# Spectral gating kernel: exchanging the spectra of two neighbouring steps in one pair of transfers

## The chip, the core and the metric

One core of one Trainium2 chip runs the kernel. The metric is the device time of one execution in microseconds (us), from the runs that are shown; three runs of the kernel before gave 118.08, 118.17 and 118.53, median 118.17.

## What is computed

The input x has 2048 rows and 1024 columns in bfloat16. Two global filters A and B are applied to it in the frequency domain, and a gate for each row mixes the two results:

```python
x = A_x                                          # [1, 2048, 1024]
g = sigmoid((x * gate_w).sum(-1, keepdims=True))
X = rfft2(x)                                     # over rows and columns, 513 columns kept
a = irfft2(X * (A_w_r + 1j * A_w_i), s=(2048, 1024))
b = irfft2(X * (B_w_r + 1j * B_w_i), s=(2048, 1024))
out = g * a + (1 - g) * b
```

Only A's x is used. Each of the four filter tensors is [2048, 513] in bfloat16.

## The kernel before

All transforms are matrix products with constant cosine and sine tables on TensorE (PE). The 2048-point transform over rows is split into 32 times 64 points.

- **Stage 1** (`stage1`, L379 and L390) makes the 32-point part, after DVE has folded x (`fold`, L340).
- **Steps 0 to 15** (`step`) take the rest of the forward transform, each for one half of the columns and two of 16 blocks of row frequencies (steps 0 to 2 and 4 to 8 the lower half, 3 and 9 to 15 the upper). `stage2(i + 2)` makes the column transform two steps ahead (PE L451 and L460, copied out of PSUM by ACT L469 or, for two steps, by DVE L467). `stage4(i)` makes the 64-point transform over rows (PE L480), and ACT L487 writes the step's spectrum to tile XF. The real and imaginary parts of one frequency lie in neighbouring partitions.
- **`swap(i)`** exchanges neighbouring partitions: two DMAs copy the spectrum from XF to tile MM, one moves even partitions to odd ones, the other odd to even, 64 rows of 2048 bytes (128 KB) each. Steps 0 to 8 issue them from POOL, steps 9 to 15 from SP. A DMA is issued through the helper `dma`, so that all are recorded at L283.
- **`product(i, kind)`** (DVE L508) multiplies the spectrum with the filters, in place in tile W. Kinds A0 and A1 read the spectrum in XF, kinds B0 and B1 the exchanged one in MM. The digit is the filter, 0 or 1. Steps 7, 8 and 11 to 15 are taken in two halves of their columns, and 11 to 14 two steps at a time.
- **Row groups** (`group`, PE L604, copied out by ACT L615 or DVE L613) take eight columns each and start the inverse transform over rows. The first ones need the products of all steps of the lower half, of which step 8 is the last, and of its columns only the first half.
- **Stages 6 and 7** (PE L754 and L783) finish the inverse, and the rows are stored.

XF holds 8 spectra in a ring, MM holds 7 exchanged ones. Step i has place (i + 1) modulo 8 in XF and place (i + 1) modulo 7 in MM. Each place has a key in the program's own dependency tracking: `r` names what an instruction reads, `w` what it overwrites, `a` what it adds to; waits are derived from these keys. All DMAs with one name share a semaphore, and whoever reads what they wrote waits for all of them. Every engine runs its instructions in the order in which the program adds them.

A step calls `stage4(i)`, then `swap(i)`, then `stage2(i + 2)`; then the products of that step's entry in `ORDER` are added. The order of products on DVE is written out by hand. Entry by entry from step 3 on it is: A0 of 3, A0 of 2 | B0 of 0, A0 of 4, A1 of 0 | B0 of 1, B1 of 0, A1 of 1 | B0 of 2, B1 of 1, A1 of 2 | B0 of 3, B1 of 2, A1 of 3 | B0 of 4, B1 of 3, A1 of 4 | A0 and B0 of 5, B1 of 4, A1 of 5 | A0 and B0 of 6, B1 of 5, A1 of 6 | first half of the columns of 7, with B1 of 6 in between | first half of 8, then the second halves of 7 and 8 | 9.

The filters are loaded from HBM by SP (`wload`, 44 DMAs at L283, the last of them for steps 8 and 15). SP issues them ahead of its own exchanges, without waits in between, and after the exchanges come the constants of the later stages. POOL issues nothing but the exchanges of steps 0 to 8 in this part of the kernel.

Of the kernel before, what the change touches and what calls it, by code (L numbers as in the profile page):

```python
# [232 lines left out]
def bass_gated_mix__spectral_gfnet__spectral_gfnet__prompt_kernel(nc, A_x, A_w_r, A_w_i, B_x, B_w_r, B_w_i, gate_w, out):  # L233
# [9 lines left out]
    XF = sb("XF", 11264)  # L243
    MM = sb("MM", 7168)
# [13 lines left out]
    def sl(t, off, dims, p0=0, np_=128, pstep=1):  # L258
        n = t.shape[1]
        return AP(t, p0 * n + off, [[n * pstep, np_]] + [list(x) for x in dims])  # L260
# [4 lines left out]
    def bank(b):  # L265
        return ("ps", b)
# [15 lines left out]
    def dma(eng, name, dst, src, **kw):  # L282
        return P.add(eng, lambda e: e.dma_start(dst, src), dma=name, **kw)  # L283
# [11 lines left out]
    for _ in range(18):  # L295
        P.add("pe", lambda e: e.matmul(ps(7 * 512, [(1, 256)]), sl(CL, GRo, [(1, 128)]), sl(CL, GRo, [(1, 256)]), start=True, stop=True),
              r=["GRz"], w=[bank(7)])
# [114 lines left out]
    last1 = [P.ops["pe"][-1]]  # L412
    SEQ = [(0, 0), (0, 1), (0, 2), (1, 0)] + [(0, p) for p in range(3, 8)] + [(1, p) for p in range(1, 8)]
    CSo = lambda i: (i % 3) * 1024
    Xk = lambda i: (i + 1) % NX
    Xo = lambda i: 3072 + Xk(i) * 1024
    XSk = lambda i: (i + 1) % NXS
    XSo = lambda i: XSk(i) * 1024
# [70 lines left out]
        return out  # L489

    def swap(i):
        eng = ("pool", "sp")[i > 8]
        for ri in range(2):
            dma(eng, f"xs{i}", sl(MM, XSo(i), [(1, 1024)], p0=1 - ri, np_=64, pstep=2), sl(XF, Xo(i), [(1, 1024)], p0=ri, np_=64, pstep=2),
                r=[("X", Xk(i))], **({"a": [("XS", XSk(i))]} if ri else {"w": [("XS", XSk(i))]}), after=last1)

    def product(i, kind, h0=0, n=2, ni=1):

# [147 lines left out]
    def step(i):  # L646
        nonlocal last2
        stage4(i)()
        swap(i)
        if i + 2 < 16:  # L650
            last2 = stage2(i + 2)
# [45 lines left out]
    groups(1)  # L697
    out15()
    swap(15)
    groups(1)  # L700
    star_column(2 * spare())
# [224 lines left out]
```

## Time and profile before

| | us |
|---|---|
| median of three runs | 118.17 |
| the profiled execution | 118.88 |
| its span, first to last instruction | 116.6 |
| PE busy | 110.0 |
| DVE busy | 100.7 |
| ACT busy | 96.5 |
| POOL busy | 34.0 |
| median from issue to landing, exchanges from POOL (18 DMAs) | 5.4 |
| median from issue to landing, exchanges from SP (14 DMAs) | 2.7 |

The mean granted clock of TensorE was 0.991. Times in what follows are us from the start of the span. A group's line gives the line of the kernel, engine, operation, tiles (out<-in) and shapes. An engine's name with a q (SPq, POOLq) is its sequencer, which waits and issues DMAs. Queue 0 holds the DMAs that POOL issues, queue 1 those of SP. A wait in square brackets is idle time of the engine just before the instruction, with what ended it. In the timeline, neighbouring instructions of one group are merged (x2), and the length is that of all of them together.

### The profile page before, as it was taken

The page shows a single profiled execution, that of the slowest core. Times are in us where ns is not written, and L with a number is a line of the kernel's source. Part 1 is how long each engine was busy: PE and PEld are TensorE (multiplying, and loading weights), DVE is VectorE, ACT ScalarE, POOL GpSimd, SP SyncE. Part 2 cuts the span into 40 slices and gives each one's busy share as a digit, 9 for nine tenths or more (in the row PEclk, how much of TensorE's full clock was granted, in tenths as well). Part 3 has the DMA queues.
Part 4 walks back from the last instruction along what each step waited for, and adds up shares of the span by engine and source line. Part 5 has one row for each costly group of instructions (what it writes and reads, how often), then busy time and mean ns, then how long its engine had stood idle before and what let it go on. Part 6 is the DMA issues. An engine that isn't in the chain of part 4 may idle for free.

```text
span 116.6 us, 4237 instructions
## 1 busy us (share of the span) xinstructions
PE 110.0 (94%) x1812; PEld 88.4 (76%) x1812; DVE 100.7 (86%) x210; ACT 96.5 (83%) x117; POOL 34.0 (29%) x43
## 2 busy tenths in 40 slices
PE   6999999999999999999999999999999999999950
PEld 4666888875766657569999999999988777777430
DVE  0478998978999999699999999999568999899990
ACT  5239998997799999939999999997879889988420
POOL 1000030016655600000000000000002999999930
PEclk9999999999999999999999999999999999999996
DMA  3999999999999999962369930000000135425466
GB/s 86 289 405 415 421 359 355 352 349 350 363 370 358 368 364 362 350 241 100 139 172 407 389 123 0 6 0 6 0 6 0 46 146 181 181 96 193 153 233 236
DMA packets 17682, 26.14 MB, mean 224 GB/s; under 512 B 2112, under 2 KB 11072, under 8 KB 17664
## 3 DMA queue, kind: packets, MB, share of 16 engines
q1 hardware_dynamic: 16368, 23.00, 56.2%
q0 software_dynamic: 864, 2.36, 5.6%
q10 hardware_dynamic: 432, 0.52, 1.4%
q8 instruction: 14, 0.23, 0.8%
q14 instruction: 4, 0.03, 0.1%
HBM read 17.48 MB, written 4.19 MB: 186 GB/s over the span
## 4 chain that ended last, share of the span: by engine, by line
PE 51%; SPq 29%; DMA 9%; DVE 3%; issue 2%; ACT 2%; DVEq 0%
SPq L283 29%; PE PS L604 26%; PE PS L783 15%; PE PS L754 7%; DMA W<-in_B_w_i_dram 6%; DMA W<-in_A_x_dram 3%; PE PS L379 2%; DVE W L508 1%; DVE MM L794 1%; ACT W L615 1%; PE PS L563 1%; ACT XF L790 1%; PE PS L582 1%; DVE XF L340 0%; DVEq L865 0%
## 5 line engine op out<-in xcount | busy, mean ns | idle before, releaser
L604 PE MATMUL PS<-CL,W 128*128 128x128 bf16 x512 | 32.3, 225 | 0.2 <-DVE W L508 0.2
L604 PEld LDWEIGHTS PS<-CL,W 128*128 128x128 bf16 x512 | 31.6, 145 | 0.9 <-DVE W L508 0.7
L835 POOL TENSOR_TENSOR MM<-FT 128x512 bf16<-128x512 f32 x14 | 17.4, 1273 | 48.7 <-DVE FT L830 48.7
L615 ACT ACTIVATE W<-PS 128x1024 bf16<-128x1024 f32 (+1 forms) x30 | 28.5, 1036 | 3.0 <-PE PS L604 2.9
L508 DVE TENSOR_TENSOR W<-XF,W 128x1024 bf16<-128x1024 bf16 (+1 forms) x38 | 22.4, 608 | 1.6 <-DMA W<-in_B_w_i_dram 0.9
L508 DVE TENSOR_TENSOR W<-MM,W 128x1024 bf16<-128x1024 bf16 (+1 forms) x38 | 22.4, 613 | 0.2
L783 PE MATMUL PS<-FT,W 128*128 128x256 bf16 (+1 forms) x132 | 19.4, 299 | 0.1
L487 ACT ACTIVATE XF<-PS 128x1024 bf16<-128x1024 f32 x16 | 17.3, 1079 | 1.6 <-PE PS L480 1.6
L480 PE MATMUL PS<-XF,CK 128*128 128x512 bf16 (+1 forms) x72 | 17.8, 357 | 0.1
L767 ACT ACTIVATE W<-PS 128x1024 bf16<-128x1024 f32 (+1 forms) x15 | 14.8, 992 | 2.7 <-PE PS L754 2.7
L340 DVE TENSOR_TENSOR XF<-W 128x512 bf16<-128x512 bf16 (+2 forms) x34 | 11.4, 404 | 5.9 <-DMA W<-in_A_x_dram 5.7
L783 PEld LDWEIGHTS PS<-FT,W 128*128 128x128 bf16 x132 | 12.1, 98 | 5.4 <-DVE XF L794 0.7
L379 PE MATMUL PS<-MM,XF 128*128 128x256 bf16 x128 | 14.9, 273 | 0.6 <-DVE XF L340 0.4
L469 ACT ACTIVATE XF<-PS 128x1024 bf16<-128x1024 f32 x14 | 15.0, 1078 | 0.1
L379 PEld LDWEIGHTS PS<-MM,XF 128*128 128x128 bf16 x128 | 12.2, 98 | 3.5 <-DVE XF L340 2.0
L390 ACT ACTIVATE FT<-PS 128x1024 bf16<-128x1024 f32 (+2 forms) x15 | 13.1, 1012 | 0.8 <-PE PS L379 0.8
L283 POOL DMA_DIRECT2D MM<-XF x18 | 9.9, 550 | 13.4 <-PE PS L480 8.0
L830 DVE TENSOR_TENSOR FT<-PS,XF 128x512 f32<-128x512 f32 x18 | 11.6, 684 | 0.8 <-ACT XF L790 0.4
L451 PEld LDWEIGHTS PS<-F,FT 128*128 128x128 bf16 x128 | 8.4, 98 | 3.1 <-ACT FT L390 0.2
L790 ACT ACTIVATE XF<-PS 128x512 f32<-128x512 f32 (+1 forms) x16 | 8.5, 533 | 2.2 <-PE PS L783 2.2
L451 PE MATMUL PS<-F,FT 128*128 128x128 bf16 x128 | 10.2, 219 | 0.0
L480 PEld LDWEIGHTS PS<-XF,CK 128*128 128x128 bf16 x72 | 4.7, 97 | 6.1 <-ACT XF L487 5.7
(62 smaller groups left out, 104.3 us busy)
## 6 DMA issues: line engine op xcount, KB each, us to landing
W<-in_A_x_dram SPq DMA_DIRECT2D x7, 512.0 KB, 7.5
out_dram<-MM SPq DMA_DIRECT2D x10, 256.0 KB, 2.5
MM<-XF POOLq DMA_DIRECT2D x18, 128.0 KB, 5.4
FT<-c_U SPq DMA_DIRECT2D x1, 2048.0 KB, 8.5
MM<-XF SPq DMA_DIRECT2D x14, 128.0 KB, 2.7
W<-in_A_w_r_dram SPq DMA_DIRECT2D x4, 256.5 KB, 6.3
W<-in_A_w_i_dram SPq DMA_DIRECT2D x4, 256.5 KB, 6.7
W<-in_B_w_r_dram SPq DMA_DIRECT2D x4, 256.5 KB, 7.1
```

Source lines behind the costliest of these rows:

```text
L283: return P.add(eng, lambda e: e.dma_start(dst, src), dma=name, **kw)
L379: P.add("pe", lambda e, o=o, lh=lh, rh=rh, s=s: e.matmul(o, lh, rh, start=(s == 0), stop=(s == 1)), r=[("xf", c % 2, q, h, s ^ j), ("M", c ...
L451: P.add("pe", lambda e, o=o, cs=cs, j=j, t=t, rh=rh: e.matmul(o, fblock(1 + cs, j, t), rh, start=(j == 0), stop=(j == 1)), r=[("F1a" if p ...
L469: P.add("act", lambda e: e.activation(dst, src, ACT.Copy), **kw)
L480: P.add("pe", lambda e, o=o, kind=kind, pm=pm, m=m, rh=rh: e.matmul(o, sl(CK, fbo(kind, pm, m), [(1, 128)]), rh, start=(m == 0), stop=(m = ...
L487: P.add("act", lambda e: e.activation(dst, src, ACT.Copy), **kw)
L508: P.add("dve", lambda e: e.tensor_tensor(out=rows((1 - h) * 64 * RP + sw * HW), in0=sl(xt, xo + 128 * h + 64 * h0, [(0, 2), (256, 4 * ni), ...
L604: P.add("pe", lambda e, o=o, l0=l0, ab=ab: e.matmul(o, sl(W, HW * ab + l0, [(RP, 128)]), sl(CL, KIo[ab], [(1, 128)]), start=(ab == 0), sto ...
L615: P.add("act", lambda e: e.activation(dst, src, ACT.Copy), r=b, a=keys)
L767: P.add("act", lambda e, s=src, d=dst: e.activation(d, s, ACT.Copy), **kw)
L783: P.add("pe", lambda e: e.matmul(ps(col, [(1, n * 256)]), lh, rh, start=(k == 0), stop=(k == last)), r=[("Y", r), "DI"] + ["DJ"] * (full o ...
L835: P.add("pool", lambda e, s=s, op=op: e.tensor_tensor(out=ods(s, 0, 2), in0=pv[:, :, 0, :], in1=pv[:, :, 1, :], op=op), r=[("PQ", pk, 0), ...
```

## The change

`swap(i)` does nothing in steps 0, 2, 4, 7, 9 and 11. In the step after each of these it exchanges the spectra of both steps, with two DMAs of 64 rows of 4096 bytes (256 KB) each, since the places of the two follow each other in both rings. Steps 6, 13, 14 and 15 are exchanged as before. There are 20 DMAs in place of 32. The issuing engine is that of the pair's first step, so that steps 0 to 8 stay with POOL and 9 to 15 with SP. The order of everything else is the same.

```diff
     def swap(i):
+
+        if i in (0, 2, 4, 7, 9, 11):
+            return
+        i, n = (i - 1, 2) if i in (1, 3, 5, 8, 10, 12) else (i, 1)
         eng = ("pool", "sp")[i > 8]
+        xs = [("XS", XSk(k)) for k in range(i, i + n)]
         for ri in range(2):
-            dma(eng, f"xs{i}", sl(MM, XSo(i), [(1, 1024)], p0=1 - ri, np_=64, pstep=2), sl(XF, Xo(i), [(1, 1024)], p0=ri, np_=64, pstep=2),
-                r=[("X", Xk(i))], **({"a": [("XS", XSk(i))]} if ri else {"w": [("XS", XSk(i))]}), after=last1)
+            dma(eng, f"xs{i}", sl(MM, XSo(i), [(1, 1024 * n)], p0=1 - ri, np_=64, pstep=2), sl(XF, Xo(i), [(1, 1024 * n)], p0=ri, np_=64, pstep=2),
+                r=[("X", Xk(k)) for k in range(i, i + n)], **({"a": xs} if ri else {"w": xs}), after=last1)
```

## The prediction

> **What bounds the kernel now.** I read the chain of waits first, then the stretch it passes through, engine by engine, then the DMA queues of that stretch. The chain (start, length, what):
>
> ```profile
> 42.62 6.80 DMA W<-in_B_w_i_dram
> ...
> 49.51 0.78 DVE W L508 x2
> ...
> 50.31 0.45 DVE W L508
> ...
> 50.78 0.45 DVE W L508
> ...
> 51.27 1.16 PE PS L604 x15
> ```
>
> The last filter weights land at 49.42. Four half-width products of step 8 follow on DVE (49.51 to 51.23), the first row group starts on PE at 51.27, and from there PE has no idle time worth the name: in the windows view PE is busy 42.92 us of the 43.00 between 53.5 and 96.5. So whatever moves the products of step 8 moves the end one for one. Now DVE's timeline, at the first product that reads an exchanged spectrum (W<-MM) and just before the weights:
>
> ```profile
> 31.88 0.69 DVE L508 TENSOR_TENSOR W<-XF,W 128x1024 bf16<-128x1024 bf16 x1
> 32.48 0.69 DVE L508 TENSOR_TENSOR W<-MM,W 128x1024 bf16<-128x1024 bf16 x1
> ...
> 47.72 0.42 DVE L508 TENSOR_TENSOR W<-XF,W 128x512 bf16<-128x512 bf16 x1
> 48.18 0.44 DVE L508 TENSOR_TENSOR W<-MM,W 128x512 bf16<-128x512 bf16 x1
> 49.51 0.42 DVE L508 TENSOR_TENSOR W<-XF,W 128x512 bf16<-128x512 bf16 x1 [0.89 <-DMA W<-in_B_w_i_dram]
> ```
>
> Between 31.28 and 48.62 DVE has no gap: its products stand back to back, and the only slack ahead of step 8 is the 0.89 us that it waits for weights. A stall of S us anywhere in that stretch costs the end S - 0.89. PE and ACT give little room in the other direction: PE's last stage 4 ends about 50.8, so the first group could start at most 0.47 us sooner than 51.27, whatever DVE and the weights do.
>
> Now the exchanges. POOL's timeline shows the issues of steps 0, 1 and 2:
>
> ```profile
> 25.76 1.22 POOL L283 DMA_DIRECT2D MM<-XF  x2 [8.04 <-PE PS L480]
> 27.29 1.08 POOL L283 DMA_DIRECT2D MM<-XF  x2 [0.31 <-ACT XF L487]
> 29.01 1.08 POOL L283 DMA_DIRECT2D MM<-XF  x2 [0.64 <-ACT XF L487]
> ```
>
> The DMA view of small windows gives the time to landing of the second transfer of step 0, then of step 1:
>
> ```profile
> MM<-XF POOLq DMA_DIRECT2D x1, 128.0 KB, 5.7
> ```
> ```profile
> MM<-XF POOLq DMA_DIRECT2D x1, 128.0 KB, 5.5
> ```
>
> Issued at 26.43 and 27.83, they landed at 32.16 and 33.31. B0 of step 0 starts at 32.48: its input has been there for only 0.32 us. The same sum for B0 of steps 1, 2, 3 and 4 (they start at 34.29, 36.12, 37.94, 39.76; inputs landed at 33.31, 34.72, 36.56, 39.25) leaves 1.0, 1.4, 1.4 and 0.5 us. Pairing holds the even step's exchange back until the odd step's spectrum is there, 1.5 to 1.8 us of POOL's timeline later. Last, the queues between 29.6 and 33.5:
>
> ```profile
> q1 hardware_dynamic: 789, 0.76, 60.2%
> q0 software_dynamic: 237, 0.66, 46.6%
> ```
>
> The two shares add to more than 100%: the DMA engines are full, and queue 0 (POOL's) moves 0.66 MB in 3.9 us, 0.17 MB per us. Queue 0 has no row in the window from 24 to 29.6, so its first packet comes some 3.9 us after the issue at 25.76.
>
> **The change, part by part.** *Fewer issues.* POOL goes from 18 issues to 10, SP from 14 to 10; at 0.54 us each that is 4.3 and 2.2 us of issue time. Neither is on the path: POOL sits idle 0.31 to 0.75 us before each exchange, waiting for ACT, and SP reaches the exchanges only at 44.45, when its last weight issue is out. Worth 0. Bytes are the same, so the weight stream keeps its 49.42, give or take 0.3 us; after a stall that is hidden behind DVE.
>
> *Exchange of steps 0 and 1.* No row shows a 256 KB transfer on queue 0. Its lower bound: it is issued when step 1's is today and carries at least the same bytes, so it lands no earlier than 33.31. Its middle: first packet 27.29 + 3.9 = 31.2; four times 131 KB are 0.52 MB; at 0.17 MB per us that takes 3.1 us, at the best burst of the rows (both transfers of step 2, 0.26 MB in 1.3 us) 2.6 us; the last packet is at 33.8 to 34.3. A transfer's landing comes 0.6 to 0.8 us after its last packet (step 1: last packet of the queue about 32.75, landed 33.31). So 34.4 to 35.0; the product starts 0.1 later (weights landed 49.42, DVE 49.51). B0 of step 0 moves from 32.48 to 34.5 to 35.1: a stall of 2.0 to 2.6 us. DVE is in order, so A0 of step 4, A1 of step 0 and every product after stand behind it, and row groups behind those.
>
> *Steps 2 and 3.* Issue at 30.84, first packet 34.7, 2.6 to 3.2 us of packets, landing 37.9 to 38.6. B0 of step 2, at 36.12 today, already stands at 38.1 to 38.7 behind the first stall: nothing more.
>
> *Steps 4 and 5.* Issue at 34.39, first packet 38.25, landing by the same sum 41.5 to 42.2; B0 of step 4, at 39.76 today, stands at 41.8 to 42.4: nothing more. But step 5's two transfers took 2.0 us of packets between 38.2 and 40.2; at twice that the landing is 43.0 and the stall grows by 0.7 to 1.3. I take the mean rate, since it is also that of 38.1 to 40.3 (0.36 MB in 2.2 us), and keep the other for the range.
>
> *Steps 7 and 8.* Issue unchanged at 39.89 (step 8 sets it; B1 of step 1, whose place it overwrites, ends at 37.42 + 2.4). Landing near 47.1, against B0 of step 7 at 46.77 + 2.4. Covered; without the first stall it would cost some 0.4.
>
> *Steps 9 to 12, on SP's queue.* Both spectra of 9 and 10 are there (43.27) before SP is free at 44.45; step 9's product reads the exchange at 55.08, 3 us after the landing of step 10's today. The pair of 11 and 12 must wait for B1 of step 5, which the stall moves to about 48.3; behind it in SP's queue are steps 13 to 15, of which 14 waits for DVE until 53.9 even today. Then come the phase constants, landed at 66.07 and first read at 75.7. All covered. ACT's write of step 14's spectrum at 49.46 needs A1 of step 6, 46.5 + 2.4: covered by 0.5 us.
>
> **Sum.** Stall S = 2.4 (middle of 2.0 to 2.6, a little up for the slow stretch at 38 to 40), less the 0.89 that DVE spends on weights anyway: +1.5 us. What is late next: PE, whose 0.47 us of waiting before the first group becomes about 2. The profiled execution (118.88, its span 116.6 and 2.3 around it) would come to 120.4; it lies 0.7 above the median 118.17, so I forecast 119.7.
>
> A rule weighed against these rows: 128 KB on queue 0 take 5.1 to 6.1 us from issue to landing here, and a pair of transfers 1.3 to 2.0 us of packets. The Trainium skill, DMA: Bandwidth & Descriptors, "Rules for kernel authors", tells to coalesce many small transfers into a large one, and "Anatomy of one DMA" gives a POOL-issued transfer 2.0 us plus its bytes by 436 KB per us, 2.3 us for 128 KB. By that, an estimate, 128 KB more cost only 0.30 us, and the end would move by some +0.3 to +0.7 instead of +1.5. The trace disagrees with the page's size of both terms, so I go by the rows; the mechanism is rival 1.
>
> **Rivals.** (1) *The second half rides almost free.* Fixed time is most of a transfer (3.9 us before the first packet, 0.7 after the last, of 5.5), and pairs fall into gaps of queue 0. Then steps 0 and 1 land where the fourth transfer does today, 33.31 (stall 0.9), steps 4 and 5 at 40.95 against 39.76 (stall 1.3): +0.4, 118.6. For it: gaps in queue 0 of up to 0.5 us between steps. Against: full engines. (2) *The issue or the slow stretch doubles too.* If a POOL issue grows from 0.54 to 1.08 with the bytes, the first packet comes at 31.7, the last about 34.9 and the landing at 35.55: stall 3.2, and steps 4 and 5 add up to 0.6: +2.3 to +2.9, 120.5 to 121.1. For it: nothing here shows an issue with longer rows; against: SP's issues hardly depend on size (0.60 us for 2048 KB of constants). (3) *Not slower.* The weights run undisturbed until 31.2 instead of 29.6, land sooner, and the group starts at PE's 50.8: at best -0.47, 117.7. It decides only if S stays under 0.89, that is if the pair has landed by 33.27, earlier than its second half lands today.
>
> **Chances.** Forecast (+0.9 to +2.1) 0.62; rival 1 0.17, rival 2 0.14, rival 3 0.07. What a measurement here can tell from no change is about 0.5%, 0.59 us. Slower by more: forecast, rival 2 and a sliver of rival 1, 0.78. Within: rival 1's rest and most of rival 3, 0.19. Faster: 0.03, since rival 3 ends at 0.4%. The range takes in rival 1 and nearly all of rival 2: 118.5 to 120.9.
>
> **What would show it.** Right: a wait of about 2 us on DVE, ended by DMA MM<-XF, before the first W<-MM product, now near 34.8; no wait for weights at 49.5; a longer wait of PE L604 for DVE W L508, the first group near 52.8; POOL with 10 issues of 0.5 to 0.7 us and landings 1 us or more above 5.4. Wrong: that product before 33.6, or a wait for weights still ahead of step 8; or the stall there and the end not moved, which would mean that the row groups had slack which the trace hides.

## The result and the profile after

The changed kernel took 121.02 us (median of six executions, 120.92 to 121.53) against 118.47 for the kernel before in the same comparison: ratio 1.0231, 95% interval 1.0203 to 1.0258, slower by 2.5 us. The forecast was 119.7, with a range to 120.9. The profiled execution took 121.02, its span was 119.2, so that 1.8 us lie outside the span, against 2.3 before. It had begun its steps 0.21 us later than the profile of before (first spectrum on ACT at 24.35 against 24.14), which is no part of the change.

DVE's timeline has two waits for exchanges where it had none, and no wait for weights any more (start, length, engine, line, tiles; in brackets the idle time before and what ended it):

```profile
34.33 0.70 DVE L513 TENSOR_TENSOR W<-MM,W 128x1024 bf16<-128x1024 bf16 x1 [1.56 <-DMA MM<-XF]
...
38.80 1.31 DVE L513 TENSOR_TENSOR W<-MM,W 128x1024 bf16<-128x1024 bf16 x2 [0.74 <-DMA MM<-XF]
...
50.86 0.44 DVE L513 TENSOR_TENSOR W<-MM,W 128x512 bf16<-128x512 bf16 x1
51.21 0.42 DVE L513 TENSOR_TENSOR W<-XF,W 128x512 bf16<-128x512 bf16 x1
```

The first is B0 of step 0, the second B0 of step 2 (with B1 of step 1 behind it). Step 8's first product, at 49.51 in before, now starts at 51.21 right behind its predecessor. POOL's timeline shows the cause. It has five pairs of issues in place of nine; the first three are those of 0-1, 2-3 and 4-5, each held back until the odd step's spectrum is there:

```profile
27.79 1.23 POOL L283 DMA_DIRECT2D MM<-XF  x2 [9.91 <-PE PS L480]
31.05 1.07 POOL L283 DMA_DIRECT2D MM<-XF  x2 [2.04 <-ACT XF L487]
34.60 1.07 POOL L283 DMA_DIRECT2D MM<-XF  x2 [2.48 <-ACT XF L487]
```

PE's timeline has the two places where the end moved:

```profile
52.49 0.28 PE L609 MATMUL PS<-CL,W 128*128 128x128 bf16 x1 [1.39 <-DVE W L513]
52.97 2.10 PE L609 MATMUL PS<-CL,W 128*128 128x128 bf16 x31 [0.20 <-DVE W L513]
...
78.39 8.97 PE L609 MATMUL PS<-CL,W 128*128 128x128 bf16 x144 [0.77 <-DVE W L618]
```

The first row group starts at 52.97 instead of 51.27: 1.70, or 1.49 without the 0.21 at the start. That is the forecast's +1.5. The second wait, 0.77 us near 78, was not in the forecast at all. The chain of waits names its way: PE waits for DVE's copy of a row group (L618), which stands behind DVE's last products.

```profile
76.77 0.43 DVE W L513
77.20 1.14 DVE W L618
78.34 0.05 issue
78.39 8.97 PE PS L609 x144
```

and DVE's timeline shows what had made DVE late there, the two small products of the star column (tile XST, the frequency column that `star_column` exchanges on SP):

```profile
62.38 0.29 DVE L560 TENSOR_TENSOR XF<-XST,W 128x64 bf16<-128x64 bf16 x2 [0.76 <-DMA XST<-XST]
```

So about 1.5 us were lost by 53 and another 0.8 us at 78; both had to be explained. Why 2-3 landed so late, why XST did, and why other executions of the changed kernel, whose XST need not be late, took as long, were the open points.

Two rows of the DMA view answer the first. Queue 0 between 34.7 and 36.85, then from 36.85 to 38.35 (packets, MB, share):

```profile
q0 software_dynamic: 158, 0.52, 63.0%
...
q8 instruction: 1, 0.02, 3.0%
```
```profile
q0 software_dynamic: 2, 0.00, 1.9%
```

158 of the pair's 160 packets were out by 36.85. Two more came late, one of data at 37.49 and one that counts up the semaphore at 38.03, and the pair landed at 38.77, 7.2 us after its issue. The one packet on queue 8 began at 36.46: 16 KB of instructions that took 1.04 us, until 37.50, just when the late data packet started. The trace names queues and no engines; that this fetch sat on the very DMA engine that still owed the last packet was a theory, to be tested by moving the fetch.

XST met another one. Its two transfers, from issue to landing, in before and after (the view of the tile):

```profile
DMA to landing us min/median/max: 1.8/1.8/1.8
```
```profile
DMA to landing us min/median/max: 1.8/2.5/3.3
```

The slow one's packets ran from 60.21 to 60.38, but for five of its 80, which came at 61.19 to 61.25; a fetch had begun at 60.20 and taken 1.0 us. In before XST's packets were out at 58.40 and the fetch came at 58.69.

### The profile page after: what moved, and what is told of

Its sections match the earlier page's. It is cut to its first block, busy times and chain, and to the rows that moved or that the text cites. A ratio compares the mean times of both kernels' runs of the same rounds, so it can differ in the third digit from the quotient of the medians.

```text
span 119.2 us, 4221 instructions
## 1 busy us (share of the span) xinstructions
PE 110.0 (92%) x1812; PEld 88.4 (74%) x1812; DVE 100.8 (85%) x210; ACT 96.5 (81%) x117; POOL 29.7 (25%) x35
## 4 chain that ended last, share of the span: by engine, by line
PE 57%; DVE 14%; DMA 12%; ACT 9%; issue 2%; SPq 2%; POOL 0%; DVEq 0%
PE PS L609 22%; PE PS L788 14%; DVE W L513 11%; PE PS L379 8%; PE PS L759 7%; DMA MM<-XF 6%; DMA W<-in_A_x_dram 6%; ACT W L620 2%; ACT XF L487 2%; ACT XF L571 2%; SPq L283 2%; ACT XF L469 2%; PE PS L480 2%; PE PS L451 1%; DVE MM L799 1%
## 5 line engine op out<-in xcount | busy, mean ns | idle before, releaser
L283 POOL DMA_DIRECT2D MM<-XF x10 | 5.5, 556 | 18.3 <-PE PS L480 9.9
```

## The experiments

All times are medians; the ratio to the kernel before, run on the same chip in the same comparison, stands beside them. "0-1" is the exchange of steps 0 and 1, and so on.

| run | waits of DVE for 0-1, 2-3, XST | clock 53 to 58 | us | ratio (95%) |
|---|---|---|---|---|
| changed kernel | 1.56, 0.74, 0.76 | 1.00 | 121.02 | 1.0231 (1.0203 to 1.0258) |
| e1, pairs on POOL only | 1.61, 0.84, 0 | 0.66 | 121.43 | 1.0221 (1.0165 to 1.0276) |
| e2, pairs on SP only | 0, 0, 0 | 1.00 | 119.28 | 1.0046 (1.0016 to 1.0075) |
| e3, star column later | 1.59, 0.92, 0 | 0.66 | 120.77 | 1.0154 (1.0076 to 1.0233) |
| e4, moved in the program | 0, 0, 0 | 1.00 | 118.56 | 1.0016 (0.9984 to 1.0047) |
| e5, PE kept busy | 1.70, 0.56, 0 | 1.00 | 120.79 | 1.0191 (1.0147 to 1.0236) |
| e6, both | 1.67, 0.67, 0 | 1.00 | 120.06 | 1.0131 (1.0085 to 1.0176) |
| e7, held, single transfers | 1.05, 0, 0 (0.20 for step 3) | 1.00 | 119.33 | 1.0047 (1.0006 to 1.0089) |
| e8, only 2-3 | 0, 2.35, 0 | 1.00 | 120.96 | 1.0206 (1.0149 to 1.0263) |
| e9, fetch later | 1.74, 0, 0 | 1.00 | 119.44 | 1.0117 (1.0027 to 1.0207) |
| e10, before, fetch later | 0, 0, 0 | 1.00 | 118.45 | 1.0008 (0.9984 to 1.0032) |
| e11, only 0-1 | 1.54, 0, 0 | 1.00 | 119.28 | 1.0063 (1.0028 to 1.0098) |
| e12, only 7-8 | 0, 0, 0 | 1.00 | 118.28 | 0.9991 (0.9966 to 1.0015) |

Waits and clock are those of one profiled execution of each.

### e1: pairs on POOL only

```diff
-        if i in (0, 2, 4, 7, 9, 11):
+        if i in (0, 2, 4, 7):
-        i, n = (i - 1, 2) if i in (1, 3, 5, 8, 10, 12) else (i, 1)
+        i, n = (i - 1, 2) if i in (1, 3, 5, 8) else (i, 1)
```

> Pairs on POOL only (0-1, 2-3, 4-5, 7-8); steps 9 to 15 one by one on SP as before. Theory: the change costs two stalls of DVE. The first (2.3 us of waits for pairs 0-1 and 2-3, less the 0.89 us that DVE spent on weights) comes from POOL's pairs: +1.5 us at the first row group, kept here. The second (0.76 us for the star column's exchange XST, 0.8 us at the end) comes from SP: with four issues fewer, SP's pause of 0.43 us that follows its ninth exchange issue falls between the two issues of step 15, just ahead of XST, and the second XST transfer then meets a 16 KB instruction fetch of 1.0 us on one DMA engine. Here SP has its 14 issues again, so the pause is back at step 13 and the second stall is gone: 1.5 us over before, about 120.0. Rival: the second stall is only a later echo of the first, then 2.5 us over before, about 121.0.

Half right. SP's pause stood between the two issues of step 13 again (the second one at 51.65, 0.44 after the first was done), XST landed 1.8 us after its issues, and neither DVE nor PE waited later on. That the pause did this is not shown, though: the fetch that met XST at 60.20 in the changed kernel came only at 65.0 here. And the time was 121.43, not 120.0. The windows view shows what took the place of the second wait (length, busy of PE, PEld, DVE, ACT, POOL, then the granted clock, DMA share, GB/s):

```profile
50.00:53.00 3.00, 1.40 (x15) 0.53 (x11) 2.90 (x8) 0.92 (x2) 0.00 (x0) 1.00 0.50 180
53.00:58.00 5.00, 4.85 (x58) 4.86 (x59) 4.86 (x14) 3.12 (x5) 0.00 (x0) 0.66 0.21 79
58.00:62.00 4.00, 4.00 (x69) 4.00 (x68) 3.90 (x9) 4.00 (x5) 0.00 (x0) 1.00 0.43 107
```

After PE had idled 1.55 us before the first row group its clock fell: 0.66 over five microseconds is 0.5 for 3.4 us, and PE started 58 matmuls there where the changed kernel's profile has 80 at a clock of 1.00. PE works 1.7 us' worth in 3.4 us; the loss at the end was about 1 us, as the executions of e3 show below. In the six executions of the changed kernel the mean clock was 0.992 in three and 0.978 to 0.985 in the other three, and all took 120.9 to 121.5. So it looks as if an execution loses about the same either way, by the clock or by XST; XST was only seen in the profiled one. The profiles suggest why it is one or the other: in the two in which the clock fell, the fetch came at 65.0 (e1) and 63.7 (e3), long after XST had landed. The Trainium skill, TensorE: Matmul & The Clock Gate, "HAM oscillation — how this bites in real kernels", asks for no idle gap of PE above some 3.4 us. The slow stretch was as long as that figure, 3.4 us; but the gap that sufficed here was 1.55 us, within a stretch (50 to 53) in which PE was busy 1.40 of 3.00.

### e2: pairs on SP only

```diff
-        if i in (0, 2, 4, 7, 9, 11):
+        if i in (9, 11):
-        i, n = (i - 1, 2) if i in (1, 3, 5, 8, 10, 12) else (i, 1)
+        i, n = (i - 1, 2) if i in (10, 12) else (i, 1)
```

> Pairs on SP only (9-10, 11-12); POOL's exchanges one by one as before. Theory: no wait for MM<-XF, first row group where it was (about 51.3); SP's pause again between the issues of step 15, XST issued about 0.4 us later than before, so that its second transfer comes at 58.6 to 58.7, where the instruction fetch came at 58.69: landing between 59.2 and 60.4 against a need at 59.84, so 0 to +0.5 us, about 118.4 to 118.9. Rival (SP's pairs do nothing at all): XST lands near 58.8, no wait, 118.4.

Its profile has no wait for an exchange; XST landed at 58.88, 1.75 us after its issue, just as the fetch came (58.88). SP's pause came one issue sooner than expected, ahead of both issues of step 15. The time was 0.5% above before, but in the profile the whole excess lies at the start, where the first spectrum was written at 24.90 instead of 24.14, before the change does anything. What 0.5% comes from stays open; it is not a wait behind the pairs.

### e3: the star column's products later

```diff
-    star_products()
     for k in range(2):
...
-        for a in fa("A0B0A1B1") + pa("A0B0") + ...
+        for a in fa("A0B0"):
+            product(*a)
+        if k == 0:
+            star_products()
+        for a in fa("A1B1") + pa("A0B0") + ...
```

> The changed kernel with all its pairs, and the two star column products (L560) on DVE 1.3 us later: after A0 and B0 of steps 11 and 12, so that XST at 62.3 is there before they are reached. Theory: no wait for XST, the wait of PE of 0.77 us for DVE's copy of a row group (L618) near 78 goes with it: about 0.8 us under the changed kernel, 120.2. Rival: that wait of PE has another cause (DVE late as a whole): 121.0.

Two executions (mean clock 0.993 and 0.995) gave 120.15 and 120.24, as expected, and two (0.984 and 0.980) 121.29 and 121.43. The profile is of the last: no wait for XST or for L618, but again the clock at 0.66 between 53 and 58, after PE had idled 1.62 us. So the first two fit a wait for XST that was worth the 0.8 us, and the clock is another loss, of some 1.1 us, that comes or doesn't.

When it comes may hang on where PE's wait lies. In each trace the clock changes only at whole multiples of 3.41 us from its first rise (in e1 1.00 lasts 14 such stretches, 0.5 one, 1.00 another 18). In the stretch that held most of the wait, PE was busy 1.66 us of 3.41 in e1 and 1.59 in e3, where the clock fell right after it, and 2.02 in the changed kernel's profile and 2.11 in e8's, where it did not. At the end of e12 a stretch with 1.45 us was not followed by a fall, and no run moved the wait against these stretches, so this is not shown.

### e4: held back by the program's order alone

```diff
+    def swap(j):
+        if j in (0, 2, 4, 7):
+            return
+        for i in ((j - 1, j) if j in (1, 3, 5, 8) else (j,)):
+            exchange(i)
```

> Steps 0 to 8 held back as in the change (step 0's exchange issued only after step 1's spectrum, and so on), but as single transfers of 128 KB with a semaphore for each step, the even step's first; SP as before. Theory that hold-back and the joint, larger transfer both count: B0 of step 0 waits only for the first two transfers, which land where step 1's do today (33.3 on the times of before): stall 0.9 us; steps 2 and 3 no more, steps 4 and 5 up to 0.4 us more; less the 0.89 us of slack: 0 to +0.4 us, about 118.4 to 118.9. Rival (holding back is all of it, size and joint semaphore nothing): +1.5 us as with pairs on POOL, 120.0.

A miss of the experiment: POOL issued step 0's exchange at 25.94, as early as in before (25.76). The call's later place in the program changes nothing on POOL, for which it is the next instruction anyway and which waits only for the spectrum. It is a run of before (ratio 1.0016). e7 made the hold real.

### e5 and e6: PE kept busy through its wait

```diff
     out15 = stage4(15)
+    for _ in range(12):
+        P.add("pe", lambda e: e.matmul(ps(7 * 512, [(1, 256)]), sl(CK, 0, [(1, 128)]), sl(CK, 0, [(1, 256)]), start=True, stop=True),
+              r=["CK"], w=[bank(7)])
     groups(1)
```

> The changed kernel with 12 matmuls of 256 columns (about 1.3 us) on PE ahead of the first row group, into a bank that the group then overwrites: they fill the 1.5 us in which PE waits for step 8. Theory: where PE idles there, the granted clock falls to 0.5 for 3413 ns in some executions (two of the four profiles with the stall), and that is worth some 1 us; where it does not fall, XST comes too late and costs 0.8 us. With the filler the clock never falls, and the wait for XST stays: 120.9 to 121.1, mean clock 0.99 in every run. Rival (the clock falls whatever PE does there): again some profile with 0.98 and a clock of 0.5 between 52 and 58.

> As e5_warm, and the two star column products 1.3 us later on DVE. Theory: both later losses are gone, what is left is the first stall alone, 2.3 us less 0.89 us and some 0.1 us: 1.5 to 1.7 us over before, 120.0 to 120.2 in every run. Rival (one of the two losses has another cause): 120.8 to 121.4 in some runs.

The clock had fallen in two of the three profiles with the stall until then, e1 and e3. e5: 119.89 in the profiled execution, in which neither the clock fell nor DVE waited for XST, and 120.6 to 120.98 in the others, with mean clocks of 0.993 to 1.0. e6, which takes away both, gave 119.58 to 120.37, median 120.06, where 120.0 to 120.2 was expected. In its profile one XST transfer took 3.1 us and cost nothing, because the products that read it came later. What is left in e6 is the stall of the exchanges alone: 1.4 us over before (118.63), 1.0 to 2.1 by the interval.

### e7: held back, but as single transfers

```diff
+        held = (i, i + 1) if i in (0, 2, 4, 7) else (i,)
...
-                r=[("X", Xk(i))], ...
+                r=[("X", Xk(k)) for k in held], ...
```

> Steps 0 to 8 with single transfers of 128 KB and a semaphore for each step, but those of steps 0, 2, 4 and 7 wait for the next step's spectrum as well (e4 had only moved them in the program, which held nothing back); SP as before. Theory that the larger, joint transfer counts beside the hold-back: B0 of step 0 waits for two transfers that land where step 1's do in before (33.3): stall 0.9 us, steps 4 and 5 up to 0.4 us more, less 0.89 us: 0 to +0.4 us, 118.4 to 118.9. Rival (the hold-back is all of it): stall 2.3 us as in the change, +1.5 us or more, 120 to 121.

119.33, 0.7 us over before (118.63). DVE's timeline of this kernel:

```profile
33.69 0.70 DVE L509 TENSOR_TENSOR W<-MM,W 128x1024 bf16<-128x1024 bf16 x1 [1.05 <-DMA MM<-XF]
...
39.44 0.70 DVE L509 TENSOR_TENSOR W<-MM,W 128x1024 bf16<-128x1024 bf16 x1 [0.20 <-DMA MM<-XF]
```

The stall was 1.25 us, near the upper end of the 0.9 to 1.3 that were expected; the time, 0.7 us over, lies above the 0 to 0.4, since it had been reckoned with 0.89 us of slack (more on this below). Of the 1.56 us that the changed kernel waits for 0-1, holding the even step back is thus 1.05, and the rest, some 0.5, goes with the common, larger transfer and its one semaphore. The changed kernel's second wait, 0.74 for 2-3, has another cause (e9).

### e8 and e11: one pair at a time

e8 pairs steps 2 and 3 only (`if i in (2,)`, `i in (3,)`), e11 steps 0 and 1 only.

> Only steps 2 and 3 in one pair, everything else one by one. Theory: the stall of the change is set by the pair that lands last against its product, and that is 2-3, whose second transfer took 7.2 us: B0 of step 2 waits some 2.3 us by itself, first row group +1.5 us, 120.0, or 121 where the clock falls. Rival (as the prediction had it: 2-3 lands at 37.9 to 38.6, and is late only through the queue behind 0-1): a stall of 1.8 us or less, +0.9 us or less, 119.3.

> Only steps 0 and 1 in one pair. Theory: wait of 1.6 us for it, all others as in before, less 0.89 us of slack: first row group 0.7 us late, 119.1 to 119.3, PE's wait there about 0.9 us and the clock at 1.0. Rival (the prediction's size for this pair, 2.0 to 2.6): 119.6 to 120.2.

e8's only wait for an exchange (DVE's timeline):

```profile
38.73 1.31 DVE L513 TENSOR_TENSOR W<-MM,W 128x1024 bf16<-128x1024 bf16 x2 [2.35 <-DMA MM<-XF]
```

One pair makes DVE wait as long as all of them do, 2.35 against 1.56 + 0.74: the second transfer of 2-3 took 7.15 us here too. So the queue behind 0-1 is not what delays it. The time, 120.96, holds the clock's loss in three of the four executions (mean clock 0.978 to 0.980). e11:

```profile
34.37 0.70 DVE L513 TENSOR_TENSOR W<-MM,W 128x1024 bf16<-128x1024 bf16 x1 [1.54 <-DMA MM<-XF]
```

1.54 us, and 119.28, 1.0 us over before (118.28). The stalls don't add up: DVE keeps its order, so what counts is the pair that lands latest against its product.

### e9 and e10: the instruction fetch moved

```diff
-    for _ in range(18):
-        P.add("pe", lambda e: e.matmul(ps(7 * 512, [(1, 256)]), ..., sl(CL, GRo, [(1, 256)]), ...
+    for _ in range(8):
+        P.add("pe", lambda e: e.matmul(ps(7 * 512, [(1, 512)]), ..., sl(CL, GRo, [(0, 2), (1, 256)]), ...
```

> The changed kernel; the 18 warm-up matmuls of 256 columns at PE's start become 8 of 512, so that PE has 20 instructions fewer ahead of the steps and its 16 KB instruction fetches come some 0.6 us later. Theory: pair 2-3 landed at 38.8 only because one DMA engine was busy with such a fetch from 36.46 for 1.04 us: 15 of 16 engines had done their part by 36.9. With the fetch at about 37.1 the pair lands near 37.6, before its product (37.9); the stall is that of pair 0-1 alone, 1.6 us, the first row group 0.7 to 0.8 us late, and XST (60.2) is off its fetch as well: 119.1 to 119.3. Rival (256 KB on a busy queue just take that long): waits for both pairs and XST as before, 121.0.

> The kernel before with the same 8 warm-up matmuls of 512 columns: the control. Theory: no exchange of before is late against its product, so moving the fetches does little: 118.4, within 0.3. Rival (the warm-up itself is worth something): off by more than 0.5.

The fetch came at 36.95 instead of 36.46, half a microsecond later and behind the pair's packets. The second transfer of 2-3 from issue to landing, in the changed kernel and in e9:

```profile
MM<-XF POOLq DMA_DIRECT2D x1, 256.0 KB, 7.2
```
```profile
MM<-XF POOLq DMA_DIRECT2D x1, 256.0 KB, 5.8
```

It landed at 37.18, and DVE has one wait left in the whole of the steps:

```profile
34.27 0.70 DVE L513 TENSOR_TENSOR W<-MM,W 128x1024 bf16<-128x1024 bf16 x1 [1.74 <-DMA MM<-XF]
```

XST landed 1.75 us after its issue, the clock stayed at 1.00, and the time was 119.44, 1.2 us over before (118.28) instead of 2.5, with every pair of the change in place (one of four executions took 120.86). The control, before with the same warm-up, was the same as before. So moving the fetches by some half a microsecond takes away, in the profile, the second wait for an exchange and both later losses. In before with the same edit (e10) the fetch meets the second transfer of step 4, which lands at 39.77 and is read at 39.95, and so it costs nothing.

Other profiles bear this out. In all six that exchange 2-3 in one pair without this edit (the changed kernel, e1, e3, e5, e6, e8), the fetch came at 36.1 to 36.8 and the second transfer took 7.2 to 7.4 us, against 5.8 here. Nor does it need a pair. In e4, which runs as before does, the fetch came at 36.02 and not at 36.26, and the second transfer of step 3, 128 KB, landed after 6.7 us instead of 5.2:

```profile
MM<-XF POOLq DMA_DIRECT2D x1, 128.0 KB, 6.7
```

That the transfer of 2-3 waits for the fetch is shown by this; which DMA engine they share is not recorded.

### e12: only steps 7 and 8

> Only steps 7 and 8 in one pair. Theory: landing near 47 at the latest, B0 of step 7 at 46.8; held back with some 0.3 us to spare or short: 118.4 to 118.7. It is the pair with the most room, so if pairs as such cost anything (longer transfers that hold up the weights), it shows here as a wait for weights above 0.9 us and a time above 118.8.

118.28, ratio 0.9991. The pair landed at 46.15, before its product. A pair costs nothing in total where its first reader is far enough, and brings nothing either. No version tried is faster than before beyond the interval.

## Why the prediction was right or wrong

The time left the forecast's range through two losses that the prediction put at nothing: SP's queue, of which it said "All covered", lost 0.8 us, and PE's longer wait, to which it gave no price, cost about 1 us by the clock; an execution seems to have one or the other. Two more terms were wrong, the slack of 0.89 and the 2.3 us around the span, and these nearly cancel. The kernel before, too, came out at 118.47 in the comparison, 0.3 above the 118.17 that the forecast started from.

**Right: what bounds the kernel, and the way to the first row group.** A stall of DVE among the products costs the row groups its length less the slack, and B0 of step 0, with 0.32 us to spare, is where it starts. Between the two profiles, 2.30 us of waits became 1.49 at the first group, near 52.8 as named. The wait before the first W<-MM product, named as 2 us, was 1.56. Rivals 1 and 3 fell. Rival 2 named a time, 120.5 to 121.1, that holds the measured 121.02, but its reasons fell too: the issue on POOL did not grow (0.54 us with rows twice as long), and no product waited for the exchange of steps 4 and 5.

**Right by two errors that cancelled: the stall of 2.4.** The term for steps 0 and 1, 2.0 to 2.6, was too large: 1.56. Its 0.52 MB took 2.0 us of packets (31.7 to 33.7), not 2.6 to 3.1: the 0.17 MB per us of queue 0 in before was what it moved with pauses between the exchanges, and the joint transfers moved 0.26. The term for steps 2 and 3, "nothing more", was too small: 0.74, and 2.35 alone (e8). The pair did land near the 37.9 to 38.6 of the sum, at 38.77, but for another reason: with the fetch out of the way it landed at 37.18 (e9).

**Wrong: "less the 0.89".** That slack was the wait for weights in one profiled execution, which at 118.88 lay 0.7 above the median. The prediction carried the 0.7 over as something constant. The profiles of e4, e10 and e12, three kernels that run as before does, show no wait for weights; there the products that the first group needs end 0.3 to 0.4 us before PE reaches it, and that is all the slack they have. In e12, on DVE and on PE:

```profile
49.84 0.44 DVE L513 TENSOR_TENSOR W<-MM,W 128x512 bf16<-128x512 bf16 x1
```
```profile
50.67 1.51 PE L609 MATMUL PS<-CL,W 128*128 128x128 bf16 x22
```

A stall of 2.3 us then costs 1.9 to 2.0. The row groups show it: from the first spectrum on ACT to the group matmuls behind the first 32, e4, e10 and e12 take 28.8 to 28.9 us and the changed kernel 30.9 (24.35 to 55.22). That is 2.0 us for 2.30 of stall, and in the same way 1.5 for 1.74 (e9), 1.2 for 1.54 (e11) and 1.0 for 1.25 (e7).

**Wrong: "2.3 around it".** The prediction took the time outside the span over unchanged. It fell by 0.4 us: in every execution of the nine kernels with a pair on POOL (the changed one, e1, e3, e5, e6, e8, e9, e11, e12) it is 1.75 to 1.93 us, and in all whose span is on record of those with POOL's 18 single transfers (before, e2, e4, e7, e10) 2.11 to 2.31. One pair is enough for it (e12), and what part of the execution it comes from is not shown. So the change has a gain after all, and e6, with the stall alone, comes out at 1.4 us over before, close to the forecast's 1.5, because the slack and this were both misjudged: that is luck.

**Wrong: "All covered" for SP's queue.** The paragraph on steps 9 to 12 followed the exchanges and the phase constants, and left out the two XST transfers between them in SP's queue, with a slack of 1.09 us (landed 58.75, read at 59.84). XST's second transfer met an instruction fetch and landed 3.3 us after its issue instead of 1.8, which made DVE wait 0.76 us; that is 0.8 us at the end. SP's pause may have brought the two together. SP pauses 0.43 us after its ninth exchange issue (in e2 after the eighth); with four issues fewer the pause falls between the issues of step 15, just ahead of XST, and no longer at step 13. Without it XST's packets would, by an estimate, have been out 0.43 us sooner, by 59.95 in place of 60.38, before the fetch at 60.20. No run shows this part by itself.

**Wrong: a longer wait of PE costs only its length.** The prediction saw PE's wait grow to about 2 us and put no price on it. In part of the executions the clock halves for 3.4 us after it, about another microsecond (e1, e3). With PE kept busy and the star column moved the time is 120.06 (e6).

Added up on the median of before: 118.5, 1.9 to 2.0 for the stall and 0.8 to 1 for one of the two later losses, less the 0.4 outside the span, give 120.8 to 121.1, against 121.02.

**The rule on coalescing**, which the prediction took from the Trainium skill, would have given +0.3 to +0.7. The prediction's estimate from the Trainium skill's figure, 0.30 us for 128 KB more, is of the size that the rows gave once the fetch was away: in e9 the second transfer of 0-1 took 6.0 us against 5.7 in before, and that of 2-3 5.8 against 5.2. What the rule leaves out is that the first spectrum has to wait for the second: e9 came out 1.2 us over before, e11 1.0.

## What to carry to other kernels

Joining two transfers makes the earlier one wait for the later one's data, so price a pair by the slack of its first reader: 0.3 us of slack cost 1.0 to 1.2 us here (e11, e9), and 1.8 us of hold-back with enough slack cost nothing (e12). Where a queue loses instructions, follow everything behind them on that queue to its reader, small transfers above all. And when PE's wait grows to what it was here, 1.4 to 1.6 us, add a price for its clock. Last, check the time outside the span before carrying it over: here it changed by 0.4 us.

## What the runs showed of the hardware that was not expected

Instruction fetches hold up data transfers: in the steps one packet of 16 KB on queue 8 came about every 9 us (27.06, 36.46 and 45.65 in the changed kernel) and took 1.0 to 1.1 us, and a transfer that met it landed some 1.5 us later (7.2 against 5.8 for 256 KB; 3.3 against 1.8 for 4 KB). Only a small part of the transfer is held up. In the trace each transfer raises its semaphore 16 times; of the second transfer of 2-3, 15 of these came by 37.35 and the last at 38.77, and of XST's, 15 by 60.71 and the last at 62.29. The Trainium skill, Runtime: NRT & Kernel Launch, "Instruction fetch mechanics", tells of blocks of 16 KB, 256 instructions, fetched by a DMA queue of the sequencer, and calls their cost mostly hidden; here 20 instructions fewer on PE moved a fetch by half a microsecond and, with it, brought the changed kernel from 2.5 to 1.2 us over before.
